# Transposes by DMA in place of TensorE, in an attention with data-dependent decay followed by a SwiGLU FFN

## The chip, the cores and the metric

One core of a Trainium2 chip runs the whole program. The metric is device time in microseconds, the median of several executions.

## The reference

```python
def _attn_ref(r, k, v, w, u):              # (4, 8, 768, 48): batch, heads, time, head size
    for t in range(S):
        cur = np.einsum('bhd,bhe->bhde', u[None] * kt, vt)
        y[:, :, t] = np.einsum('bhd,bhde->bhe', rt, state + cur)
        state = wt[:, :, :, None] * state + np.einsum('bhd,bhe->bhde', kt, vt)

def _moe_ref(x, w_gate, w_val, w_out, rms_g):   # x: (3072, 384); d_ff = 1536
    rms = np.sqrt(np.mean(x * x, axis=-1, keepdims=True) + 1e-06)
    xn = x / rms * rms_g
    g = xn @ w_gate
    silu = g * (1.0 / (1.0 + np.exp(-g)))
    return silu * (xn @ w_val) @ w_out
```

The attention's y, with time and heads put in order (token, head x size), is the FFN's x.

## The kernel before

Time is cut into six blocks of 128 steps (m or n = 0 to 5); each block holds four batches (j = 0 to 3). One batch of one block is a tile with the 128 steps on the partitions and 8 heads x 48 on the free axis. Inside a block the recurrence is done in parallel form: sums of log decay by a matmul with a triangular mask (`cs_mm`), their exponential (`cs_exp`), r and k multiplied by it (`r_mul`, `k_mul`, into bf16 tiles padded to 64 per head so that two heads fill 128 columns), the 128 x 128 products q = k r^T for each head (`q_mm`), masked to earlier steps (`q_mask`), and y = q v + r state (`y_mm`). The diagonal term with u is computed apart: GpSimd multiplies r, k and u (`bonus_mul`), VectorE sums over the head (`bonus_sum`), GpSimd multiplies by v (`bonus_v`), and `x_add` puts it to y. `st_mm` and `st_new` carry the state to the next block.

Products over the head's 48 elements need r and k with the head on the partitions, so `tr_mm` transposes them on TensorE (eight 128 x 128 pieces, two heads each) into PSUM, and ScalarE (`tr_r`) and VectorE (`tr_k`) copy them to `rkT`. In the same way x, once normalised (`x_sq`, `x_rstd` on GpSimd, `xn_mul` with rms_g on VectorE), is transposed in three pieces by `xn_mm` and copied by `xn_out` into `xnt`, the FFN's input for the four batches of a block (512 tokens).

The FFN of block n has 12 steps f (`gv_mm`: six matmuls of 512 columns, `silu` on ScalarE, `h_mul` on VectorE) and four output steps (`o_mm`, 12 matmuls each, `o_out`). PSUM is in three pools of two buffers each: `psG` for cs and gate/value, `psQ` for q and the output, `psT` for transposes, state, y.

The order of all work is a hand-written plan: each operation is entered by `at(time, fn, ...)` with a planned time, the list is sorted, and the operations are issued in that order; every engine and every DMA queue then runs its own part in order, and waits by semaphores. The planned times set the order only. FFN stage n has 16 slots; blocks 0 and 1 are done in a head ahead of FFN 0, and block m from 2 on is done beside FFN m-1, its preparation (cs, r, k, transposes) in the last slots of FFN m-2. The inputs are fp32 and reach SBUF by SP's queue (`load`, L92), in pools of two buffers per input; the weights are cast on the way by GpSimd's queue (`load_gv`, `load_wo`); outputs leave by SP's queue.

Of the kernel before, what the change touches and what calls it, by code (L numbers as in the profile page):

```python
# [25 lines left out]
def kernel(  # L26
# [97 lines left out]
    nc.vector.memset(rA.rearrange("p a b h d -> p (a b h) d")[:, :, D:PD], 0.0)  # L124
    nc.vector.memset(kA.rearrange("p a b h d -> p (a b h) d")[:, :, D:PD], 0.0)
# [57 lines left out]
    def r_mul(n, j):  # L183
        nc.vector.tensor_tensor(out=rA[:, n % 2, j, :, 0:D], in0=inp[n, "r"][:, j],  # L184
                                in1=ewk[n, j][:, 4:4 + DM].rearrange("p (h d) -> p h d", h=H), op=ALU.mult)

    def k_mul(n, j, eng):
        eng.tensor_tensor(out=kA[:, n % 2, j, :, 0:D], in0=inp[n, "k"][:, j],  # L188
                          in1=ewk[n, j][:, 4 + DM:4 + 2 * DM].rearrange("p (h d) -> p h d", h=H),
                          op=ALU.mult)  # L190
# [17 lines left out]
    def tr_mm(n, j):  # L208
        ps = bank["tr", n, j] = psT.tile([128, 2 * NP, 128], BF16, name="ps_t")
        for q in range(NP):  # L210
            nc.tensor.transpose(ps[:, q, :], pair(rA[:, n % 2, j], q), ident)
        for q in range(NP):
            nc.tensor.transpose(ps[:, NP + q, :], pair(kA[:, n % 2, j], q), ident)
        rkT[n, j] = pt.tile([128, 2 * NP, 128], BF16, name="rkT", bufs=5)

    def tr_r(n, j):
        nc.scalar.copy(out=rkT[n, j][:, 0:NP, :], in_=bank["tr", n, j][:, 0:NP, :])  # L217

    def tr_k(n, j):
        nc.vector.tensor_copy(out=rkT[n, j][:, NP:, :], in_=bank["tr", n, j][:, NP:, :])  # L220
# [13 lines left out]
    def q_mask(n, j, half):  # L234
        nc.vector.tensor_tensor(out=qts[n, j][:, half], in0=bank["q", n, j][half],  # L235
                                in1=bc_mid(mask_lt, NP), op=ALU.mult)
# [17 lines left out]
    def y_mm(n, j):  # L254
        if n not in xb:
            xb[n] = pt.tile([128, SB, DM], BF16, name="xb")
            rstd[n] = pt.tile([128, 2, SB], FP32, name="rstd")
        ps = bank["y", n, j] = psT.tile([128, DM], FP32, name="ps_t")
        t, q = rkT[n, j], qts[n, j]
        if n > 0:  # L260
            for i in range(NP):
                nc.tensor.matmul(ps[:, i * 2 * D:(i + 1) * 2 * D], lhsT=t[:, i, :],
                                 rhs=st[:, n % 2, j, i, :], start=(i == 0), stop=False)
        for h in range(H):
            nc.tensor.matmul(ps[:, h * D:(h + 1) * D], lhsT=q[:, h % 2, h // 2, :],  # L265
                             rhs=vb[n][:, j, h, :], start=(n == 0 and h == 0), stop=(h == H - 1))

    def x_add(n, j):
        nc.vector.tensor_tensor(out=xb[n][:, j], in0=bank.pop(("y", n, j)),  # L269
                                in1=ydiag[n][:, j].rearrange("p h d -> p (h d)"), op=ALU.add)  # L270

    def x_sq(n, j):
        nc.scalar.activation(out=junk, in_=xb[n][:, j], func=AF.Square, accum_out=rstd[n][:, 0, j:j + 1])  # L273

    def x_rstd(n, j):
        ss = rstd[n][:, 0, j:j + 1]
        nc.gpsimd.tensor_scalar(out=ss, in0=ss, scalar1=1.0 / DM, scalar2=eps, op0=ALU.mult, op1=ALU.add)
        nc.gpsimd.tensor_tensor(out=rstd[n][:, 1, j:j + 1], in0=ss, in1=mhalf, op=ALU.pow)  # L278

    def xn_mul(n, j):  # L280
        xn = bank["xn", n, j] = pt.tile([128, DM], BF16, name="xn")
        nc.vector.scalar_tensor_tensor(out=xn, in0=xb[n][:, j], scalar=rstd[n][:, 1, j:j + 1],  # L282
                                       in1=g_bc, op0=ALU.mult, op1=ALU.mult)

    def xn_mm(n, j):
        if n not in xnt:
            xnt[n] = pt.tile([128, KC, TS], BF16, name="xnt")
        ps = bank["xt", n, j] = psT.tile([128, KC, 128], BF16, name="ps_t")
        xn = bank.pop(("xn", n, j))
        for c in range(KC):  # L290
            nc.tensor.transpose(ps[:, c, :], xn[:, c * 128:(c + 1) * 128], ident)  # L291

    def xn_out(n, j):
        nc.scalar.copy(out=xnt[n][:, :, j * L:(j + 1) * L], in_=bank.pop(("xt", n, j)))  # L294
# [35 lines left out]
    HEAD = 4.0  # L330
    SLOT = 1.95
    P = 16 * SLOT
    T0 = 3.0 + 8 * HEAD + 4.0

    for m in range(2):
        for j in range(SB):
            t = 3.0 + HEAD * (m * SB + j)
            for i, which in enumerate("wkrv"):
                at(-10 + 0.1 * (m * SB + j) + 0.01 * i, load, m, which, j, 1)
            at(t, ln, m, j, 1)  # L340
            at(t + 0.9, cs_mm, m, j)
# [12 lines left out]
            at(t + 5.0, q_mask, m, j, 1)
            at(t + 5.2, st_mm, m, j)
            at(t + 6.5, y_mm, m, j)
            at(t + 6.7, st_new, m, j)
            at(t + 7.3, x_add, m, j)
            at(t + 7.9, x_sq, m, j)
            at(t + 8.4, x_rstd, m, j)  # L360
            at(t + 9.1, xn_mul, m, j)
            at(t + 9.6, xn_mm, m, j)
            at(t + 9.8, xn_out, m, j)
    at(3.0 + 5 * HEAD, load_gv, 0)
    at(3.0 + 6 * HEAD, load_gv, 1)
    at(3.0 + 7 * HEAD, load_gv, 2)
    at(3.0 + 7 * HEAD + .1, load_wo, 0)
    at(3.0 + 7 * HEAD + .2, load_wo, 1)
    at(3.0 + 7 * HEAD + .3, load_wo, 2)

    for m in range(2, NSB):
        b = T0 + (m - 1) * P
        for i, which in enumerate("wkrv"):
            at(b - 34 * SLOT + 0.01 * i, load, m, which)
        if m == 2:
            at(b - 4 * SLOT - 0.5, ln, m)
            shift, bonus = 0.6, -6
        else:
            at(b - 17 * SLOT + 1.2, ln, m)
            shift, bonus = 0.0, -14  # L380
        at(b - 8 * SLOT, cast_v, m)
        for j in range(SB):
            t = b + (-4 + j) * SLOT + shift
            at(t, cs_mm, m, j)
            at(t + 0.5, cs_exp, m, j)
            at(t + 1.4, r_mul, m, j)
            at(t + 1.4, k_mul, m, j, nc.gpsimd)
            t = b + (bonus + 2 * j) * SLOT
            at(t, bonus_mul, m, j)
            at(t + 3.0, bonus_sum, m, j)  # L390
            at(t + 3.6, bonus_v, m, j)
            t = b + (-2 + j) * SLOT + 0.1
            at(t, tr_mm, m, j)
            at(t + 0.6, tr_r, m, j)
            at(t + 0.6, tr_k, m, j)
            t = b + (1 + 3 * j) * SLOT
            at(t, q_mm, m, j)
            at(t + 0.6, q_mask, m, j, 0)
            at(t + 1.2, q_mask, m, j, 1)
            if m < NSB - 1:  # L400
                at(t + 0.1, st_mm, m, j)
                at(t + 1.8, st_new, m, j)
            t = b + (3 + 3 * j) * SLOT
            at(t, y_mm, m, j)
            at(t + 0.9, x_add, m, j)
            at(t + 1.8, x_sq, m, j)
            at(t + 2.3, x_rstd, m, j)
            t = b + (5 + 3 * j) * SLOT
            at(t, xn_mul, m, j)
            at(t + 0.8, xn_mm, m, j)  # L410
            at(t + 1.4, xn_out, m, j)

    for n in range(NSB):
        b = T0 + n * P
        for f in range(FC):
            t = b + f * SLOT + 0.3
            at(t, gv_mm, n, f)
            at(t + 1.3, silu, n, f)
            at(t + 1.9, h_mul, n, f)
        for j in range(SB):  # L420
            t = b + (FC + j) * SLOT + 0.3
# [35 lines left out]
```

## Time and profile before

| what | value |
|---|---|
| median of 3 runs | 282.22 us (280.76 to 282.44) |
| the profiled execution | 283.02 us, span 281.2 us |
| mean granted TensorE clock | 0.994 |
| TensorE busy | 216.8 us (77%) |
| VectorE, ScalarE, GpSimd busy | 176.9, 136.0, 115.4 us |
| SP's and ScalarE's DMA packets (q1) | 23.60 MB, 42.1% of 16 engines' span |
| GpSimd's DMA packets (q0) | 3.54 MB, 7.9% |

The shares are averages over a head, five stages with attention or a part of it, and a last stage without; a line of a group reads: line, engine, operation, out<-in, count, then busy time and mean ns of one, then the idle time of the engine just before these instructions and what ended it. A row of the timeline reads: start, duration, engine, line. Matmuls overlap, so the distance between starts, not a duration, is what one costs TensorE.

### The profile page before, as it was taken

The page shows a single profiled execution, that of the slowest core. Times are in us where ns is not written, and L with a number is a line of the kernel's source. Part 1 is how long each engine was busy: PE and PEld are TensorE (multiplying, and loading weights), DVE is VectorE, ACT ScalarE, POOL GpSimd, SP SyncE. Part 2 cuts the span into 40 slices and gives each one's busy share as a digit, 9 for nine tenths or more (in the row PEclk, how much of TensorE's full clock was granted, in tenths as well). Part 3 has the DMA queues.
Part 4 walks back from the last instruction along what each step waited for, and adds up shares of the span by engine and source line. Part 5 has one row for each costly group of instructions (what it writes and reads, how often), then busy time and mean ns, then how long its engine had stood idle before and what let it go on. Part 6 is the DMA issues. An engine that isn't in the chain of part 4 may idle for free.

```text
span 281.2 us, 4404 instructions
## 1 busy us (share of the span) xinstructions
PE 216.8 (77%) x1668; PEld 119.1 (42%) x1688; DVE 176.9 (63%) x306; ACT 136.0 (48%) x240; POOL 115.4 (41%) x155
## 2 busy tenths in 40 slices
PE   1355554435899598777998878998779999999994
PEld 0233333323343354333564334664336644554352
DVE  4477777857344235988766788648886578723430
ACT  2344443422445937335666355683447654524420
POOL 2555556592400377566272582644653301110000
PEclk9999999999999979999999999999999999999999
DMA  6999999999990060990069900110000200020002
GB/s 127 200 206 216 187 216 218 206 193 185 219 188 0 0 140 3 224 197 0 0 143 211 211 0 1 59 56 2 0 0 30 85 3 0 2 84 29 2 28 84
DMA packets 106821, 27.81 MB, mean 99 GB/s; under 512 B 99632, under 2 KB 106800, under 8 KB 106800
## 3 DMA queue, kind: packets, MB, share of 16 engines
q1 hardware_dynamic: 102528, 23.60, 42.1%
q0 software_dynamic: 3984, 3.54, 7.9%
q10 hardware_dynamic: 288, 0.39, 0.6%
q8 instruction: 13, 0.21, 0.3%
q14 instruction: 8, 0.07, 0.1%
HBM read 26.35 MB, written 4.72 MB: 110 GB/s over the span
## 4 chain that ended last, share of the span: by engine, by line
PE 34%; DVE 26%; ACT 13%; POOL 8%; SPq 8%; issue 8%; DMA 1%; ACTq 0%; POOLq 0%; DVEq 0%
PE ps_q L317 15%; PE ps_g L303 9%; SPq L92 8%; DVE qts L235 7%; DVE ht L311 6%; DVE xn L282 5%; ACT sg L72 4%; ACT L70 3%; PE ps_t L265 3%; DVE st L250 3%; DVE xb L269 2%; PE ps_t L291 2%; ACT lw L72 2%; POOL ydiag L205 2%; DVE diag L201 2%
## 5 line engine op out<-in xcount | busy, mean ns | idle before, releaser
L311 DVE TENSOR_TENSOR ht<-ps_g,sg 128x512 bf16<-128x512 f32 x72 | 49.5, 690 | 43.5 <-ACT sg L72 43.0
L72 ACT ACTIVATE sg<-ps_g 128x512 bf16<-128x512 f32 x72 | 43.1, 598 | 49.9 <-PE ps_g L303 43.2
L303 PE MATMUL ps_g<-xnt,wg_sb 128*128 128x512 bf16 x203 | 58.3, 385 | 5.1 <-DVE ht L311 3.6
L303 PE MATMUL ps_g<-xnt,wv_sb 128*128 128x512 bf16 x209 | 58.5, 386 | 0.2
L317 PE MATMUL ps_q<-wo_sb,ht 128*128 128x384 bf16 x288 | 51.5, 332 | 3.0 <-DVE ht L311 3.0
L205 POOL TENSOR_TENSOR ydiag<-vt,diag 128x384 f32<-128x384 f32 x24 | 19.9, 830 | 68.1 <-DVE diag L201 67.9
L317 PEld LDWEIGHTS <-ht 128*128 128x128 bf16 x288 | 27.9, 99 | 21.1 <-DVE ht L311 3.4
L235 DVE TENSOR_TENSOR qts<-ps_q,mask_lt 128x512 bf16<-128x512 f32 x48 | 31.4, 683 | 5.6 <-PE ps_q L230 5.6
L303 PEld LDWEIGHTS <-wv_sb 128*128 128x128 bf16 x216 | 21.4, 99 | 26.5 <-issue 1.7
L303 PEld LDWEIGHTS <-wg_sb 128*128 128x128 bf16 x216 | 20.1, 99 | 25.7 <-issue 9.7
L282 DVE SCALAR_TENSOR_TENSOR xn<-xb,rstd,g_bc 128x384 bf16<-128x384 bf16 x24 | 23.5, 978 | 10.3 <-POOL rstd L278 10.1
L294 ACT COPY xnt<-ps_t 128x384 bf16<-128x384 bf16 x24 | 11.5, 479 | 37.7 <-PE ps_t L291 37.7
L188 POOL TENSOR_TENSOR kA<-kt,ewk 128x384 bf16<-128x384 f32 x16 | 18.7, 1171 | 24.6 <-ACT ewk L72 24.5
L72 ACT ACTIVATE ewk<-ps_g 128x772 f32<-128x772 f32 x24 | 19.5, 813 | 18.6 <-PE ps_g L176 18.5
L184 DVE TENSOR_TENSOR rA<-rt,ewk 128x384 bf16<-128x384 f32 x24 | 18.0, 748 | 15.8 <-ACT ewk L72 10.9
L291 PE MATMUL ps_t<-ident,xn 128*128 128x128 bf16 x72 | 9.4, 249 | 23.9 <-DVE xn L282 23.5
L197 POOL TENSOR_TENSOR ruk<-rt,kt 128x384 f32<-128x384 f32 x24 | 24.9, 1038 | 6.8 <-DMA rt<-in_r_dram 6.8
L198 POOL TENSOR_TENSOR ruk<-ruk,u_bc 128x384 f32<-128x384 f32 x24 | 25.7, 1070 | 1.9
L273 ACT ACTIVATE junk<-xb 128x384 bf16<-128x384 bf16 x24 | 12.5, 519 | 14.1 <-DVE xb L269 14.0
L228 PE MATMUL ps_q<-rkT 48*128 48x128 bf16 x96 | 11.3, 247 | 10.2 <-DVE rkT L220 9.7
L220 DVE COPY rkT<-ps_t 128x512 bf16<-128x512 bf16 x24 | 10.1, 422 | 14.2 <-ACT rkT L217 14.0
L291 PEld LDWEIGHTS <-xn 128*128 128x128 bf16 x72 | 4.9, 106 | 32.7 <-DVE xn L282 32.1
(53 smaller groups left out, 294.7 us busy)
## 6 DMA issues: line engine op xcount, KB each, us to landing
out_dram<-ob SPq DMA_DIRECT2D x24, 192.0 KB, 1.9
wt<-in_w_dram SPq DMA_DIRECT2D x4, 768.0 KB, 6.6
kt<-in_k_dram SPq DMA_DIRECT2D x4, 768.0 KB, 7.6
rt<-in_r_dram SPq DMA_DIRECT2D x4, 768.0 KB, 10.4
vt<-in_v_dram SPq DMA_DIRECT2D x4, 768.0 KB, 9.0
wt<-in_w_dram SPq DMA_DIRECT2D x8, 192.0 KB, 3.7
kt<-in_k_dram SPq DMA_DIRECT2D x8, 192.0 KB, 3.9
rt<-in_r_dram SPq DMA_DIRECT2D x8, 192.0 KB, 3.8
```

The source lines that it names most:

```text
L72: nc.scalar.activation(**kw)
L92: nc.sync.dma_start(out=dst, in_=src(t, n, b0, nb))
L188: eng.tensor_tensor(out=kA[:, n % 2, j, :, 0:D], in0=inp[n, "k"][:, j], in1=ewk[n, j][:, 4 + DM:4 + 2 * DM].rearrange("p (h d) -> p h d", ...
L197: nc.gpsimd.tensor_tensor(out=ruk[n][:, j], in0=inp[n, "r"][:, j], in1=inp[n, "k"][:, j], op=ALU.mult)
L198: nc.gpsimd.tensor_tensor(out=ruk[n][:, j], in0=ruk[n][:, j], in1=u_bc, op=ALU.mult)
L205: nc.gpsimd.tensor_tensor(out=ydiag[n][:, j], in0=inp[n, "v"][:, j], in1=diag[n][:, j].to_broadcast([128, H, D]), op=ALU.mult)
L235: nc.vector.tensor_tensor(out=qts[n, j][:, half], in0=bank["q", n, j][half], in1=bc_mid(mask_lt, NP), op=ALU.mult)
L282: nc.vector.scalar_tensor_tensor(out=xn, in0=xb[n][:, j], scalar=rstd[n][:, 1, j:j + 1], in1=g_bc, op0=ALU.mult, op1=ALU.mult)
L291: nc.tensor.transpose(ps[:, c, :], xn[:, c * 128:(c + 1) * 128], ident)
L303: nc.tensor.matmul(ps[:, half * 512:(half + 1) * 512], lhsT=wt[:, c, f * 128:(f + 1) * 128], rhs=xnt[n][:, c, :], start=(c == 0), stop=(c ...
L311: nc.vector.tensor_tensor(out=ht[n][:, f, :], in0=bank.pop(("gv", n, f))[:, 512:1024], in1=bank.pop(("sg", n, f)), op=ALU.mult)
L317: nc.tensor.matmul(ps, lhsT=ht[n][:, f, j * L:(j + 1) * L], rhs=wo_sb[:, f, :], start=(f == 0), stop=(f == FC - 1))
```

## The change

- The r/k transposes go to the DMA engines: r and k share one tile `rk`, and one `dma_start_transpose` per batch (`rk_tr`) writes `rkT` from SBUF to SBUF. `tr_mm`, `tr_r` and `tr_k` are gone.
- The x transposes too (`xn_tr`). In block 0 both kinds are issued from ScalarE's queue, later from SP's.
- rms_g is no longer multiplied along the free axis. x is scaled by its rms on ScalarE (`xn_mul`), transposed, and then multiplied in `xnt` by rms_g as one number per partition (`xn_gain`, three instructions per block on VectorE). rms_g is loaded as 128 x 3 in place of a broadcast to 128 x 384.
- The mask of the odd heads: ScalarE copies q from PSUM (`q_copy_o`) and GpSimd zeroes in place what is not earlier (`q_mask_o`). The even heads' mask stays on VectorE.
- x (`xb`) is kept in fp32 in four buffers, one for each batch; before it was bf16.
- The plan: only block 0 is done ahead of FFN 0, block m from 1 on beside FFN m-1. From block 2 on the inputs are loaded per batch, four loads for each input. FFN slots are planned at 1.65 and output slots at 2.6, before all at 1.95.

```diff
-    rA = persist.tile([128, 2, SB, H, PD], BF16)
-    kA = persist.tile([128, 2, SB, H, PD], BF16)
+    rk = persist.tile([128, 2, SB, 2, H, PD], BF16)
...
-    def tr_mm(n, j):
-        ps = bank["tr", n, j] = psT.tile([128, 2 * NP, 128], BF16, name="ps_t")
-        for q in range(NP):
-            nc.tensor.transpose(ps[:, q, :], pair(rA[:, n % 2, j], q), ident)
-        for q in range(NP):
-            nc.tensor.transpose(ps[:, NP + q, :], pair(kA[:, n % 2, j], q), ident)
+    def rk_tr(n, j, eng=None):
         rkT[n, j] = pt.tile([128, 2 * NP, 128], BF16, name="rkT", bufs=5)
-
-    def tr_r(n, j):
-        nc.scalar.copy(out=rkT[n, j][:, 0:NP, :], in_=bank["tr", n, j][:, 0:NP, :])
-
-    def tr_k(n, j):
-        nc.vector.tensor_copy(out=rkT[n, j][:, NP:, :], in_=bank["tr", n, j][:, NP:, :])
+        (eng or nc.sync).dma_start_transpose(rkT[n, j], rk[:, n % 2, j].rearrange("p c h d -> p (c h d)"))
...
-    def q_mask(n, j, half):
-        nc.vector.tensor_tensor(out=qts[n, j][:, half], in0=bank["q", n, j][half],
+    def q_mask_e(n, j):
+        nc.vector.tensor_tensor(out=qts[n, j][:, 0], in0=bank["q", n, j][0],
                                 in1=bc_mid(mask_lt, NP), op=ALU.mult)
+
+    def q_copy_o(n, j):
+        nc.scalar.copy(out=qts[n, j][:, 1], in_=bank["q", n, j][1])
+
+    def q_mask_o(n, j):
+        nc.gpsimd.affine_select(out=qts[n, j][:, 1], in_=qts[n, j][:, 1], compare_op=ALU.is_gt, fill=0.0,
+                                base=0, pattern=[[0, NP], [1, 128]], channel_multiplier=-1)
...
     def x_add(n, j):
-        nc.vector.tensor_tensor(out=xb[n][:, j], in0=bank.pop(("y", n, j)),
+        xb[n, j] = pt.tile([128, DM], FP32, name="xb", bufs=4)
+        nc.vector.tensor_tensor(out=xb[n, j], in0=bank.pop(("y", n, j)),
                                 in1=ydiag[n][:, j].rearrange("p h d -> p (h d)"), op=ALU.add)
...
     def xn_mul(n, j):
-        xn = bank["xn", n, j] = pt.tile([128, DM], BF16, name="xn")
-        nc.vector.scalar_tensor_tensor(out=xn, in0=xb[n][:, j], scalar=rstd[n][:, 1, j:j + 1],
-                                       in1=g_bc, op0=ALU.mult, op1=ALU.mult)
-
-    def xn_mm(n, j):
+        xn = bank["xn", n, j] = pt.tile([128, DM], BF16, name="xn", bufs=3)
+        nc.scalar.activation(out=xn, in_=xb[n, j], func=AF.Copy, scale=rstd[n, j][:, 1:2])
+
+    def xn_tr(n, j, eng=None):
         if n not in xnt:
             xnt[n] = pt.tile([128, KC, TS], BF16, name="xnt")
-        ps = bank["xt", n, j] = psT.tile([128, KC, 128], BF16, name="ps_t")
-        xn = bank.pop(("xn", n, j))
-        for c in range(KC):
-            nc.tensor.transpose(ps[:, c, :], xn[:, c * 128:(c + 1) * 128], ident)
-
-    def xn_out(n, j):
-        nc.scalar.copy(out=xnt[n][:, :, j * L:(j + 1) * L], in_=bank.pop(("xt", n, j)))
+        (eng or nc.sync).dma_start_transpose(xnt[n][:, :, j * L:(j + 1) * L], bank.pop(("xn", n, j)))
+
+    def xn_gain(n, c):
+        nc.vector.tensor_scalar(out=xnt[n][:, c, :], in0=xnt[n][:, c, :], scalar1=gT[:, c:c + 1],
+                                scalar2=None, op0=ALU.mult)
...
-    for m in range(2):
-        for j in range(SB):
-            t = 3.0 + HEAD * (m * SB + j)
...
+    for j in range(SB):
+        t = 3.0 + 4.0 * j
...
+        at(t + 3.3, rk_tr, 0, j, nc.scalar)
...
+        at(t + 11.4, xn_tr, 0, j, nc.scalar)
...
+                    at(slot(m - 3, i * SB + j) if m > 2 else 30.0 + 4 * i + j, load, m, which, j, 1)
...
+            at(slot(m - 1, x) + 4.0, xn_tr, m, j)
+        for c in range(KC):
+            at(slot(m, 0) - 0.5, xn_gain, m, c)
```

What moves in the issue order is seen best on SP's queue. Before, it held loads alone up to the first output; the rows are the end of the loads of block 1 (8 heads each: one batch), blocks 2 and 3 (32: all four batches) and the first output:

```order
L92 DMA vt<-in_v_dram 128x8x48
L92 DMA wt<-in_w_dram 128x32x48
L92 DMA kt<-in_k_dram 128x32x48
L92 DMA rt<-in_r_dram 128x32x48
L92 DMA vt<-in_v_dram 128x32x48
L92 DMA wt<-in_w_dram 128x32x48
L92 DMA kt<-in_k_dram 128x32x48
L92 DMA rt<-in_r_dram 128x32x48
L92 DMA vt<-in_v_dram 128x32x48
L327 DMA out_dram<-ob 128x384
```

Of the change, the same queue in the second half of FFN 0: loads of r and v of block 3, the four x transposes of block 1 (L281), the first two r/k transposes of block 2 (L208) and the first outputs:

```order
L281 DMA_TRANSPOSE xnt<-xn 128x3x128
L92 DMA kt<-in_k_dram 128x8x48
L92 DMA rt<-in_r_dram 128x8x48 x2
L281 DMA_TRANSPOSE xnt<-xn 128x3x128
L92 DMA rt<-in_r_dram 128x8x48 x2
L92 DMA vt<-in_v_dram 128x8x48
L281 DMA_TRANSPOSE xnt<-xn 128x3x128
L92 DMA vt<-in_v_dram 128x8x48
L318 DMA out_dram<-ob 128x384
L208 DMA_TRANSPOSE rkT<-rk 128x8x128
L92 DMA vt<-in_v_dram 128x8x48
L318 DMA out_dram<-ob 128x384
```

The piece goes on with the second r/k transpose of block 2, the last x transpose of block 1 and the last load of block 3:

```order
L208 DMA_TRANSPOSE rkT<-rk 128x8x128
L281 DMA_TRANSPOSE xnt<-xn 128x3x128
L92 DMA vt<-in_v_dram 128x8x48
L318 DMA out_dram<-ob 128x384
L208 DMA_TRANSPOSE rkT<-rk 128x8x128
```

All of block 2's loads and 15 of block 3's 16 stand ahead of the x transpose that completes FFN 1's input; before, that transpose was no DMA.

On VectorE, at the end of a stage, the last rows of FFN 2 and the first product of FFN 3 (`ht`) before:

```order
L184 TENSOR_TENSOR rA<-rt,ewk 128x8x48
L323 COPY ob<-ps_q 128x384
L184 TENSOR_TENSOR rA<-rt,ewk 128x8x48
L282 SCALAR_TENSOR_TENSOR xn<-xb,rstd,g_bc 128x384
L220 COPY rkT<-ps_t 128x512
L184 TENSOR_TENSOR rA<-rt,ewk 128x8x48
L323 COPY ob<-ps_q 128x384
L220 COPY rkT<-ps_t 128x512
L184 TENSOR_TENSOR rA<-rt,ewk 128x8x48
L220 COPY rkT<-ps_t 128x512
L311 TENSOR_TENSOR ht<-ps_g,sg 128x512
```

and in the change at the same place:

```order
L182 TENSOR_TENSOR rk<-rt,ewk 128x8x48
L199 TENSOR_REDUCE diag<-ruk 128x8
L314 COPY ob<-ps_q 128x384
L182 TENSOR_TENSOR rk<-rt,ewk 128x8x48 x2
L314 COPY ob<-ps_q 128x384
L182 TENSOR_TENSOR rk<-rt,ewk 128x8x48
L284 TENSOR_SCALAR xnt<-xnt,gT 128x512 x3
L302 TENSOR_TENSOR ht<-ps_g,sg 128x512
```

The copies of `rkT` and the products `xn` are gone from VectorE, and the three gains stand last in the stage, ahead of everything that VectorE does for the next one.

More of the change, by code (lines that the diff above doesn't have):

```diff
@@ L364 @@
[L364 to L381, printed above, removed]
-        for j in range(SB):
-            t = b + (-4 + j) * SLOT + shift
+    FS, OS = 1.65, 2.6
@@ new lines @@
+    for c in range(KC):
+        at(T0 - 0.5, xn_gain, 0, c)
+    for i, which in enumerate("wkrv"):
+        at(15.0 + i, load, 1, which)
+    at(15.0, load_gv, 0)
+    at(31.0, load_gv, 1)
+    at(36.0, load_gv, 2)
+    for g in range(3):
+        at(40.0 + g, load_wo, g)
+    for m in range(1, NSB):
+        if m > 1:
+            for i, which in enumerate("wkrv"):
+                for j in range(SB):
+                    at(slot(m - 3, i * SB + j) if m > 2 else 30.0 + 4 * i + j, load, m, which, j, 1)
+        at(22.0 if m == 1 else slot(0, 11.9) if m == 2 else slot(m - 3, 15.5), ln, m)
+        at(slot(m - 1, -6 if m > 1 else 0.5), cast_v, m)
+        for j in range(SB):
+            t = slot(m - 1, -4 + j) if m > 1 else 24.0 + 2 * j
@@ L396 @@
[L396 to L399, printed above, removed]
-            if m < NSB - 1:
[L401 to L409, printed above, removed]
@@ L426 @@
+    for _, _, fn, args in plan:
         fn(*args)
```

144 lines of the change are left out of this document (85 added, 59 removed).

## The prediction

> **What bounds the kernel now.** I read the span by slices first, then the TensorE timeline for the start of each FFN stage, then the stages one by one: which resource is full, and who waits for whom. From the page, the span and the DMA row of the 40 slices (7.03 us each); under it the 82.7 us that this row shows full, as a table by stage:
>
> ```profile
> span 281.2 us, 4404 instructions
> DMA  6999999999990060990069900110000200020002
> ...
> core 0: us, PE busy (x) PEld busy (x) DVE busy (x) ACT busy (x) POOL busy (x), PEclk, DMA share, GB/s
> 1.70:84.40 82.70, 45.04 (x357) 26.40 (x359) 53.00 (x89) 32.10 (x64) 39.24 (x54) 1.00 1.12 201
> ```
>
> Until 84.4 us the 16 DMA engines are full (share 1.12: packets of two queues overlap), while no compute engine is busy for more than 53.0 of 82.7 us. Now the first gate/value matmul of each of the six FFN stages (TensorE timeline):
>
> ```profile
> 71.02 1.06 PE L303 MATMUL ps_g<-xnt,wg_sb 128*128 128x512 bf16 x2 [0.22 <-issue]
> 107.65 0.81 PE L303 MATMUL ps_g<-xnt,wg_sb 128*128 128x512 bf16 x2
> 147.83 0.59 PE L303 MATMUL ps_g<-xnt,wg_sb 128*128 128x512 bf16 x2
> 185.81 0.59 PE L303 MATMUL ps_g<-xnt,wg_sb 128*128 128x512 bf16 x2
> 223.41 0.59 PE L303 MATMUL ps_g<-xnt,wg_sb 128*128 128x512 bf16 x2
> 252.28 0.81 PE L303 MATMUL ps_g<-xnt,wg_sb 128*128 128x512 bf16 x2
> ```
>
> So the kernel is a head of 71.0 us (blocks 0 and 1), a stage of 36.6 (FFN 0), three stages that carry a block's attention beside the FFN (40.2, 38.0, 37.6), one that carries half of it (28.9) and one that is FFN alone (28.9). For the stage from 185.8, the same table, who TensorE waited for, and the groups of instructions that the change touches:
>
> ```profile
> 185.40:223.00 37.60, 32.90 (x288) 18.53 (x290) 28.02 (x50) 20.97 (x39) 18.86 (x24) 1.00 0.06 22
> ...
> PE ps_t L291 <- DVE xn L282: 3.5, 3, 1.7
> PE ps_g L303 <- DVE ht L311: 0.9, 1, 0.9
> ...
> L235 DVE TENSOR_TENSOR qts<-ps_q,mask_lt 128x512 bf16<-128x512 f32 x8 | 5.3, 681 | 0.0
> L282 DVE SCALAR_TENSOR_TENSOR xn<-xb,rstd,g_bc 128x384 bf16<-128x384 bf16 x4 | 3.8, 952 | 1.5 <-POOL rstd L278 1.4
> L205 POOL TENSOR_TENSOR ydiag<-vt,diag 128x384 f32<-128x384 f32 x4 | 3.3, 831 | 10.6 <-DVE diag L201 10.6
> L72 ACT ACTIVATE sg<-ps_g 128x512 bf16<-128x512 f32 x12 | 7.2, 599 | 8.3 <-PE ps_g L303 5.4 <-DVE diag L201 2.0 <-PE ps_t L265 0.9
> L217 ACT COPY rkT<-ps_t 128x512 bf16<-128x512 bf16 x4 | 2.3, 587 | 0.0
> L294 ACT COPY xnt<-ps_t 128x384 bf16<-128x384 bf16 x4 | 1.9, 479 | 6.3 <-PE ps_t L291 6.3
> L220 DVE COPY rkT<-ps_t 128x512 bf16<-128x512 bf16 x4 | 1.7, 422 | 2.6 <-ACT rkT L217 2.6
> ```
>
> Here TensorE is busy 32.9 of 37.6 us, and its largest wait, 3.5 us, is for the normalised x. DMA is idle (0.06). Two kernels in one, then: up to 84 us the queue is the scarce thing, after it TensorE.
>
> **The change, part by part.** *The steady stage.* TensorE loses eight r/k transposes and three x transposes for each of four batches. Their price is the distance between starts:
>
> ```profile
> 182.15 0.33 PE L291 MATMUL ps_t<-ident,xn 128*128 128x128 bf16 x3
> 182.32 0.33 PE L171 MATMUL ps_g<-lw,mask_lt 128*128 128x384 bf16 x1
> ...
> 182.75 0.38 PE L211 MATMUL ps_t<-ident,rA 128*128 128x128 bf16 x4
> 182.97 0.39 PE L213 MATMUL ps_t<-ident,kA 128*128 128x128 bf16 x4
> 183.19 2.11 PE L317 MATMUL ps_q<-wo_sb,ht 128*128 128x384 bf16 x12
> ```
>
> That is 0.17 us for three and 0.44 for eight, 4 x 0.61 = 2.4 us a stage. The wait of 3.5 us for xn goes with the x transposes, since nothing on TensorE reads xn any more. What is late next is xn_gain: three VectorE multiplications over 128x512 stand between the last x transpose's landing and the next stage's first matmul. No such instruction is in the trace; the nearest is the 128x512 copy of L220, 0.42 us, so 3 x 0.42 = 1.3 us at most, and nothing if the transpose lands early. I charge 1.3. The stage becomes 37.6 - 2.4 - 3.5 + 1.3 = 33.0 us; its ends are 31.7 and, if the new waits eat everything, 37.6.
>
> The other engines: VectorE drops four masks (2.7), xn (3.8) and the k copies (1.7), 8.2 of 28.0 us; it was not the bound and I credit nothing beyond the wait above. ScalarE drops 2.3 + 1.9 us of copies and takes four 128x512 copies of the odd masks (0.6 each by L72) and four scalings of x (nearest row below, 0.50): 4.2 against 4.4, no change. GpSimd takes four selects over 128x512; the one in the trace is a quarter of that:
>
> ```profile
> L160 ACT CAST vb<-vt 128x384 bf16<-128x384 f32 x8 | 4.0, 504 | 1.8 <-DMA vt<-in_v_dram 1.8
> L104 POOL TENSOR_SCALAR_AFFINE_SELECT mask_lt<-mask_lt 128x128 bf16<-128x128 bf16 x1 | 0.3, 294 | 0.1
> ```
>
> Between 0.29 and 4 x 0.29 = 1.18 us each, so GpSimd goes from 18.9 to at most 23.6 us of 33: hidden by its idle time. If that cover fails, y_mm waits behind the select (rival B). x in fp32 changes the width of one operand in three instructions of 0.5 us: nothing, or a few tenths either way.
>
> *The two last stages.* FFN 4 loses 4 x 0.17 us of transposes and takes the three gains, 29.5; of the four masks (0.68) and four xn (0.95) that leave VectorE there I credit 1.5, so 28.0. FFN 5 stays 28.9.
>
> *The head and FFN 0.* Only block 0 is left ahead of FFN 0. In the kernel before, block 0's fourth batch had its r ready here, and the first batch's x reached xnt 13.6 us after its r:
>
> ```profile
> 9.06 0.56 DVE L184 TENSOR_TENSOR rA<-rt,ewk 128x384 bf16<-128x384 f32 x1 [4.93 <-DMA rt<-in_r_dram]
> 22.71 0.48 ACT L294 COPY xnt<-ps_t 128x384 bf16<-128x384 bf16 x1 [0.97 <-PE ps_t L291]
> 28.98 0.55 DVE L184 TENSOR_TENSOR rA<-rt,ewk 128x384 bf16<-128x384 f32 x1
> ```
>
> So the compute of block 0 would allow FFN 0 at 29.0 + 13.6 = 42.6 us, 46 with some delay from transposes on ScalarE's queue, and FFN 1 at 46 + 33 to 37, about 80. **This is where the gain shrinks.** The last x transpose of block 1, without which FFN 1 cannot start, stands on SP's queue behind the loads of all of block 2 and of block 3 but the last one (the order pieces in the section on the change show it). Those loads, blocks 0 and 1 and the weights are what kept the DMA engines full until 84.4 us. Less one 192 KB load and the broadcast of rms_g, plus two 192 KB stores that now stand ahead of it, the bytes are the same; and ahead of it stand 10 transposes of r/k and 8 of x, 3/8 as large: 13 r/k transposes' worth. The DMA answers for 0 to 85 us:
>
> ```profile
> q1 hardware_dynamic: 66176, 12.59, 80.4%
> q0 software_dynamic: 3984, 3.54, 26.2%
> ...
> wt<-in_w_dram SPq DMA_DIRECT2D x8, 192.0 KB, 3.7
> ```
>
> No transpose by DMA is in the trace. By pieces: the loads moved 64 x 192 KB in 0.804 x 85 = 68.3 us, 1.07 us for 1024 pieces of 192 bytes (66176 packets / 64); an r/k transpose reads 8 x 128 = 1024 pieces of 256 bytes. As the low end, nothing at all (its packets lie beside another queue's); as the high end, 3.7 us, the landing time of a 192 KB load, as if nothing overlapped. I take 1.07, the row that has its number of pieces: 13 x 1.07 = 13.9 us. FFN 1's x is there at 84.4 + 13.9 + 1.3 (gains) = 99.6 us, some 18 us after FFN 0's own work ends, and TensorE comes to it from idleness, which costs at the start of FFN 0 before:
>
> ```profile
> 71.87 1.49 PE L303 MATMUL ps_g<-xnt,wv_sb 128*128 128x512 bf16 x3
> 78.11 0.81 PE L303 MATMUL ps_g<-xnt,wv_sb 128*128 128x512 bf16 x3
> ```
>
> Three matmuls take 0.7 us longer there, over the first four such groups: about 2.5 us, although the granted clock reads 1.00 up to 84 us.
>
> The Trainium skill has two rules on that term that do not agree (the other stands at rival C). Its page "Advanced Engine Details and Errata", X-Bar Transpose (TRN2), says that such transposes run as fast as plain DMAs, at 350 to 400 GB/s: as an estimate 0.7 us for 256 KB, and the sum would be 5 us lower. No run here shows it yet.
>
> **The sum.** 99.6 + 2.5 + 3 x 33.0 + 28.0 + 28.9 = 258.0 us of span. The profiled execution took 283.02 us beside its span of 281.2, so 1.8 us lie around it: 259.8, say 260. It was 0.8 us above the median of 282.22 and 0.6 above the slowest of the three runs shown; I leave that.
>
> **Rivals.** *A: the queue does not bind.* The transposes lie beside the loads and xn_gain beside the output matmuls. Then FFN 1 starts when the same bytes have landed, 84.4 + 1.3, no idleness precedes it, and the stages take 31.7: 85.7 + 95.1 + 28 + 28.9 = 237.7, with 1.8 about 240. For it: share 1.12 shows that queues overlap. Against: the 82.7 us are full as they stand.
>
> *B: the stage keeps its length.* ScalarE's copy and GpSimd's select now stand in series before y_mm, and GpSimd is a queue in order: it sat 10.6 us of the stage waiting for diag (L205), and a select behind such a wait is late. If it costs TensorE what xn cost, the stages stay at 37.6: 260 + 3 x 4.6 = 274. Against: two matmul slots lie between q_mm and y_mm.
>
> *C: slower than before.* An r/k transpose costs the queue over 2.5 us. Beyond the first stretch, FFN 1 and FFN 2 each need 16 loads (17.1 us), 4 stores (about 4) and 5.5 transposes' worth: more than 33 us from 2.2 us a transpose on. From 1.07 to 2.2 the total rises by 13 a us, to 274.5; from there by 13 + 11 = 24 a us, and passes 283 at 2.55. At 3.7 us it is 274.5 + 1.5 x 24 = 310. For it: 3.7 us is what a smaller load takes to land. Against: at 1.07 us a load, 3.7 us is three to four of them in a row, so the landing counts those ahead. The Trainium skill's page "VectorE: DVE Perf Modes", The three transpose paths, gives 1309 ns for one 128x128 tile by DMA; eight in a row would be, as an estimate, 10.5 us, beyond this rival's whole range. No row here can say whether tiles overlap.
>
> **How the numbers follow.** My sum 0.52 (its own range 248 to 270, for a transpose at 0.3 to 1.8 us and stages of 32 to 34.5); A 0.2; B 0.14; C 0.14, of which 0.03 ends within 1%. A range that leaves out under 2 in 10 runs from 238 to 280. Faster by over 1% (about what a measurement here can tell from no change) 0.87, within 1% 0.03, slower 0.1.
>
> **What would show it.** The DMA row full to about 100 us; a hole in TensorE ahead of FFN 1, ended by VectorE's gain, which waited for DMA; stage starts 33 us apart from there; no TensorE wait for xn; the r/k transposes near 1 us of packet time each. Wrong would be a full DMA row throughout (C), a y_mm that waits for GpSimd (B), or FFN 1 at 86 us (A).

## The result, and the profile after

The changed kernel takes 273.91 us (median of 4 runs, 272.06 to 275.85) beside 282.27 for the kernel before in the same comparison: ratio 0.972 (0.964 to 0.979). It is faster, as forecast, but by 8.4 us in place of 22. Of the runs below, two (block 0 on TensorE, unread transposes) had one slower execution in four, which their medians leave out. The profiled execution took 272.06 us, span 270.3. From its page, TensorE, the granted clock and the DMA row in 40 slices of 6.76 us:

```profile
span 270.3 us, 4039 instructions
...
PE   0123315286729104969799999999999999999994
...
PEclk9999999999977755999999999999999999999999
DMA  6999999799999998699655999969200850120002
```

Before, the DMA row was full to 84.4 us; now it is full, with one dent, to 101 us (slices 1 to 14), and TensorE has a hole of three slices (13 to 15) inside FFN 0, not ahead of FFN 1. The granted clock reads 0.7 and then 0.5 from 74 to 108 us, ahead of and inside that hole, and is full again at FFN 1. The first gate/value matmuls of the six stages on TensorE's timeline (start, duration, in brackets the idle time and what ended it):

```profile
53.65 0.58 PE L294 MATMUL ps_g<-xnt,wg_sb 128*128 128x512 bf16 x1 [3.35 <-DVE xnt L284]
...
119.13 0.90 PE L294 MATMUL ps_g<-xnt,wg_sb 128*128 128x512 bf16 x3 [2.61 <-DVE xnt L284]
...
152.76 0.90 PE L294 MATMUL ps_g<-xnt,wg_sb 128*128 128x512 bf16 x3 [0.56 <-DVE xnt L284]
...
183.92 0.90 PE L294 MATMUL ps_g<-xnt,wg_sb 128*128 128x512 bf16 x3 [0.56 <-DVE xnt L284]
...
215.07 0.90 PE L294 MATMUL ps_g<-xnt,wg_sb 128*128 128x512 bf16 x3 [0.55 <-ACT ob L316]
...
241.97 0.81 PE L294 MATMUL ps_g<-xnt,wg_sb 128*128 128x512 bf16 x3
```

The stages last 65.5, 33.6, 31.2, 31.2, 26.9 and, to the end, 28.3 us. From FFN 1 on everything is as forecast or better; FFN 1 itself starts 11.5 us **later** than before (119.1 against 107.65), where the forecast had 99.6. TensorE's waits from 45 to 120 us (in all, times, longest), and then the chain of what ended last from 94 to 119 us:

```profile
PE ps_g L169 <- ACT lw L72: 17.1, 2, 16.4
PE ps_q L216 <- DMA rkT<-rk: 8.9, 2, 5.9
PE ps_g L294 <- DVE xnt L284: 6.7, 4, 3.3
```
```profile
94.51 4.70 DMA vt<-in_v_dram
...
100.69 0.59 ACT sg L72
...
102.27 1.28 ACT L70
103.57 1.49 ACT lw L72
...
106.01 3.02 PE ps_q L308 x12
...
109.82 1.95 PE ps_q L308 x12
...
116.05 2.65 DMA xnt<-xn
118.72 0.36 DVE xnt L284
```

This is a chain that the forecast did not have. ScalarE casts block 2's v (L158) ahead of the last two silus of FFN 0 and of the ln for block 2 (`lw`, the logarithm of its decay). The cast waited 13.6 us for the last of that v to land, and with it waited all of ScalarE's queue:

```profile
99.31 1.47 ACT L158 CAST vb<-vt 128x1536 bf16<-128x1536 f32 x1 [13.62 <-DMA vt<-in_v_dram]
```

TensorE's queue stood in turn at block 2's cs (L169), which the plan puts ahead of the output matmuls. So the four output steps began at 106, and FFN 1 19.8 us after the cast.

### The profile page after: what moved, and what is told of

Same layout as the page of the kernel before. It is cut to its first block, busy times and chain, and to the rows that moved or that the text cites. A ratio compares the mean times of both kernels' runs of the same rounds, so it can differ in the third digit from the quotient of the medians.

```text
span 270.3 us, 4039 instructions
## 1 busy us (share of the span) xinstructions
PE 192.5 (71%) x1424; PEld 98.7 (37%) x1424; DVE 139.4 (52%) x247; ACT 137.0 (51%) x234; POOL 133.6 (49%) x183
## 4 chain that ended last, share of the span: by engine, by line
PE 43%; DMA 21%; POOL 10%; ACT 8%; DVE 8%; SPq 5%; issue 4%; ACTq 0%; DVEq 0%; POOLq 0%
PE ps_g L294 22%; DMA rkT<-rk 15%; PE ps_q L308 13%; SPq L92 4%; DVE ht L302 3%; PE ps_q L216 3%; DMA xnt<-xn 2%; ACT sg L72 2%; POOL rk L186 2%; DMA wt<-in_w_dram 2%; DMA vt<-in_v_dram 2%; ACT vb L158 2%; POOL ruk L195 2%; POOL ruk L196 2%; DVE rk L186 1%
## 5 line engine op out<-in xcount | busy, mean ns | idle before, releaser
L72 ACT ACTIVATE sg<-ps_g 128x512 bf16<-128x512 f32 x72 | 42.9, 596 | 53.7 <-PE ps_g L294 53.7
L294 PE MATMUL ps_g<-xnt,wg_sb 128*128 128x512 bf16 x216 | 61.6, 392 | 11.2 <-DVE xnt L284 7.9
L308 PEld LDWEIGHTS <-ht 128*128 128x128 bf16 x288 | 28.4, 99 | 18.5 <-issue 1.4
L169 PE MATMUL ps_g<-lw,mask_lt 128*128 128x384 bf16 x24 | 9.2, 385 | 35.7 <-ACT lw L72 33.9
L294 PEld LDWEIGHTS <-wg_sb 128*128 128x128 bf16 x216 | 19.1, 99 | 31.9 <-issue 11.6
L195 POOL TENSOR_TENSOR ruk<-rt,kt 128x384 f32<-128x384 f32 x24 | 24.0, 999 | 13.5 <-DMA rt<-in_r_dram 12.3
L223 DVE TENSOR_TENSOR qts<-ps_q,mask_lt 128x512 bf16<-128x512 f32 x24 | 16.4, 683 | 27.3 <-PE ps_q L218 22.3
L230 POOL TENSOR_SCALAR_AFFINE_SELECT qts<-qts 128x512 bf16<-128x512 bf16 x24 | 16.0, 668 | 27.7 <-ACT qts L227 27.7
L182 DVE TENSOR_TENSOR rk<-rt,ewk 128x384 bf16<-128x384 f32 x24 | 18.2, 762 | 21.0 <-ACT ewk L72 20.9
L271 POOL TENSOR_SCALAR rstd<-rstd 128x1 f32<-128x1 f32 x24 | 5.7, 237 | 46.9 <-ACT junk L267 46.4
L186 POOL TENSOR_TENSOR rk<-kt,ewk 128x384 bf16<-128x384 f32 x20 | 24.1, 1210 | 4.8 <-ACT ewk L72 4.7
L72 ACT ACTIVATE ewk<-ps_g 128x772 f32<-128x772 f32 x24 | 19.4, 813 | 10.1 <-PE ps_g L174 9.8
L227 ACT CAST qts<-ps_q 128x512 bf16<-128x512 f32 x24 | 13.9, 579 | 15.8 <-PE ps_q L218 13.7
L216 PEld LDWEIGHTS <-rkT 48*128 48x128 bf16 x96 | 6.0, 102 | 32.3 <-DMA rkT<-rk 24.2
L199 DVE TENSOR_REDUCE diag<-ruk 128x8 f32<-128x384 f32 x24 | 13.1, 546 | 8.9 <-POOL ruk L196 8.9
```

The costliest lines, as they stand in the source:

```text
L72: nc.scalar.activation(**kw)
L182: nc.vector.tensor_tensor(out=rk[:, n % 2, j, 0, :, 0:D], in0=inp[n, "r"][:, j], in1=ewk[n, j][:, 4:4 + DM].rearrange("p (h d) -> p h d", ...
L186: eng.tensor_tensor(out=rk[:, n % 2, j, 1, :, 0:D], in0=inp[n, "k"][:, j], in1=ewk[n, j][:, 4 + DM:4 + 2 * DM].rearrange("p (h d) -> p h d ...
L195: nc.gpsimd.tensor_tensor(out=ruk[n][:, j], in0=inp[n, "r"][:, j], in1=inp[n, "k"][:, j], op=ALU.mult)
L216: nc.tensor.matmul(qe[:, i, :], lhsT=t[0:D, NP + i, :], rhs=t[0:D, i, :], start=(i == 0), stop=(i == NP - 1))
L223: nc.vector.tensor_tensor(out=qts[n, j][:, 0], in0=bank["q", n, j][0], in1=bc_mid(mask_lt, NP), op=ALU.mult)
```

## The experiments

Two theories came first. **Packet time** (P; in later expectations volume or queue time): the transposes cost more time of the DMA queue than the 1.07 us charged. **Order** (O): FFN 0 cannot end before loads for which its own queues wait, so too many bytes stand ahead of FFN 1. After the first four runs a third was set against packet time: **blocking**, that a transpose which waits for its operands holds the loads behind it in SP's queue.

For several runs the transposes of some blocks were put back on TensorE, with the copies of the kernel before; a transpose whose PSUM buffer would not be free at its place in the plan is issued at the next place where it is:

```diff
+    def plan_rk(t, n, j, eng=None):
+        if PE_RK(n):
+            at(t, tr_mm, n, j)
+            at(t + 0.6, tr_r, n, j)
+            at(t + 0.6, tr_k, n, j)
+        else:
+            at(t, rk_tr, n, j, eng)
...
-            at(t + 2.9, rk_tr, m, j)
+            plan_rk(t + 2.9, m, j)
```

`plan_x` does the same for x. The runs, with the start of FFN 0 and FFN 1 in the profiled execution and the cast of block 2's v where it waited for its DMA:

| kernel | median us | ratio to before (95%) | FFN 0 | cast | FFN 1 |
|---|---|---|---|---|---|
| changed | 273.91 | 0.972 (0.964 to 0.979) | 53.7 | 99.31 | 119.1 |
| all on TensorE | 274.73 | 0.972 (0.967 to 0.977) | 52.8 | 80.57 | 103.0 |
| blocks 0, 1 on TensorE | 254.56 | 0.901 (0.898 to 0.905) | 52.8 | 80.25 | 99.4 |
| cast late | 270.38 | 0.958 (0.954 to 0.962) | 55.8 | moved | 115.4 |
| block 3's loads late | 285.81 | 1.014 (1.008 to 1.019) | 56.4 | 90.63 | 110.3 |
| block 1 on TensorE | 259.47 | 0.920 (0.917 to 0.924) | 62.9 | no wait | 105.4 |
| block 0 on TensorE | 262.22 | 0.927 (0.920 to 0.935) | 46.2 | 88.75 | 108.1 |
| blocks 0, 1 on TensorE, cast late | 248.53 | 0.881 (0.877 to 0.885) | 52.9 | moved | 93.7 |
| old order, by DMA | 283.91 | 1.007 (1.004 to 1.009) | 89.0 | – | 123.6 |
| unread transposes | 265.82 | 0.943 (0.936 to 0.951) | 56.7 | 91.26 | 110.1 |
| unread copies | 260.17 | 0.924 (0.918 to 0.930) | 55.6 | 86.47 | 105.7 |
| x by DMA | 256.29 | 0.911 (0.906 to 0.916) | 51.7 | 82.10 | 101.5 |
| block 1 by ScalarE's queue | 272.17 | 0.966 (0.960 to 0.972) | 56.6 | 95.92 | 119.3 |

**All transposes on TensorE** (`PE_RK` and `PE_X` true for all n; new order, masks and gains kept).

> The new plan, the new masks and gains, but every transpose back on TensorE (two psT buffers, copies by ScalarE and VectorE). Two theories of why FFN 1 started at 119.1 us and not at 99.6. P (packet time): the transposes take 1.5 us of the DMA engines and up to 2.4 beside other queues, not 1.07, and 13 r/k transposes' worth stand ahead of FFN 1's x. O (order): FFN 0 cannot finish before the loads that its own rows wait for (the cast of block 2's v stands ahead of the last two silus on ScalarE), and blocks 1 to 3 and the weights are too many bytes ahead of it. P expects FFN 1 at about 100 us, stages from there of 34 to 36 (2.4 us of transposes and a new copy each): 262 to 268 in all. O expects FFN 1 at 110 to 119 and a total of 272 to 282.

274.73 us, what the changed kernel takes: in this order moving the transposes was worth nothing in all. It gives 5.4 us in each of the stages FFN 2 and 3 (36.6 to 31.2) and loses 16.2 us ahead of FFN 1. What made the kernel faster than before is the new order with its masks and gains. P had the start of FFN 1 nearly right (103.0 for about 100) and the total wrong, since FFN 1 takes 40.3 us and the next two 36.6, not 34 to 36. O had the total, but by a start at 110 to 119 that did not come: luck.

**Blocks 0 and 1 on TensorE** (`n < 2`).

> Only blocks 0 and 1 are transposed on TensorE, 8 r/k and 8 x transposes fewer on the queues until FFN 1; blocks 2 to 5 by DMA as in the change. P expects FFN 1 at about 101 us and the stages unchanged at 31 to 34: 253 to 258 in all. O expects FFN 1 at 110 to 119: 264 to 274.

Both halves at once: 254.56 us. FFN 1 starts 19.8 us earlier, and FFN 2 and 3 take 31.2 each, as P expected and O did not. But FFN 1 does not start at 85.7, where the forecast's bytes alone would have put it. ScalarE's cast in this kernel:

```profile
80.25 1.47 ACT L158 CAST vb<-vt 128x1536 bf16<-128x1536 f32 x1 [4.71 <-DMA vt<-in_v_dram]
```

The v is there at 80.25, near the end of the full queue before (84.4); FFN 1 follows 19.1 us later. So the transposes delay v by 19.1 us, and the order theory is right about another 19 us behind it.

**The cast late.**

```diff
-        at(slot(m - 1, -6 if m > 1 else 0.5), cast_v, m)
+        at(slot(m - 1, (-0.2 if m == 2 else -6) if m > 1 else 0.5), cast_v, m)
```

> The change, with one operation moved in the plan: the cast of block 2's v, which waited until 99.3 us for its load with two silus of FFN 0 behind it on ScalarE, comes at the end of FFN 0 in place of slot 10. O expects the output matmuls of FFN 0 to start near 92 instead of 105.8 us and FFN 1 at 104 to 110: 255 to 265 in all. P expects little: the last x transpose of block 1 stands behind the same packets, FFN 1 at 115 or later, 268 to 274.

The output steps begin at 91.3 in place of 106, as O expected, yet FFN 1 gains only 3.8 us, as P expected:

```profile
115.35 1.46 PE L294 MATMUL ps_g<-xnt,wg_sb 128*128 128x512 bf16 x3 [12.90 <-DVE xnt L284]
```

That is the wait that the forecast had in mind, for block 1's x behind SP's queue: the last x was ready at 102.0, and SP issued its transpose at 112.1. In the changed kernel both chains end within 4 us of each other, so either alone buys little.

**Block 3's loads late** (its 16 loads moved from FFN 0 into FFN 1, its ln and bonus after them).

> The change, with block 3's 16 loads (17 us of queue by the 1.07 of the loads before) moved from FFN 0 into FFN 1, and its log and bonus to the places that block 2 has relative to its stage. If bytes ahead of FFN 1's input are what counts, whichever theory, FFN 1 comes 6 us earlier (six of these loads stand ahead of block 2's v) to 15 us earlier (15 stand ahead of the last x transpose): 104 to 113 us, and FFN 2 starts 33 to 38 us later if the loads hide there: 255 to 270 in all. Slower than 274 if block 3's late loads hold up FFN 1 as block 2's did FFN 0.

v is there at 90.63, 8.7 us earlier, and FFN 1 at 110.3, as expected; but the loads do not hide. FFN 1 takes 51.9 us and FFN 2 34.8, since the cast of block 3's v now waits on ScalarE inside FFN 1, as block 2's did in FFN 0:

```profile
142.95 1.47 ACT L158 CAST vb<-vt 128x1536 bf16<-128x1536 f32 x1 [13.88 <-DMA vt<-in_v_dram]
```

The bytes are put off, not saved.

**Block 1 alone, block 0 alone on TensorE** (`n == 1`, `n == 0`).

> The changed kernel with the transposes of block 1 alone on TensorE (four of r and k, four of x); block 0 and blocks 2 to 5 by DMA. Both blocks together gave back 19.8 us of the start of FFN 1 (119.1 to 99.4). Volume theory: what counts is how much queue time the transposes take, whichever block they belong to. Half of them is gone, so FFN 1 starts near 109 and the time is 263 to 265. Blocking theory: a transpose that waits for its own operands holds SP's queue in order, and the loads of block 2 and 3 stand behind it; block 1's transposes are the ones on SP's queue, block 0's are on ScalarE's. Then nearly all comes back: FFN 1 at 99 to 103, time 254 to 258.

> The mirror image: only block 0's transposes on TensorE, those of block 1 still on SP's queue. Volume theory: FFN 1 starts near 109, time 263 to 265, as with block 1 alone. Blocking theory: FFN 1 starts at 115 to 119, time 270 to 274, and only the start of FFN 0 gains (53.7 to about 52).

Each gives over half: FFN 1 at 105.4 and 108.1, together 24.8 us for the 19.8 of both. The run with block 0 decides: blocking had 115 to 119 there, so it is not the whole cause. The run with block 1 lies between the theories, 2.4 us from the 103 of blocking and 3.6 from the 109 of volume, so a part of it stays possible. TensorE's waits up to the start of FFN 0 with block 1 alone on TensorE show what else block 0's transposes cost, since FFN 0 starts at 62.9 there and at 52.8 with block 0's on TensorE too:

```profile
PE ps_q L216 <- DMA rkT<-rk: 14.4, 4, 6.9
```

TensorE waits for the landing in all four batches of block 0.

**Blocks 0 and 1 on TensorE, and the cast late.**

> Blocks 0 and 1 transposed on TensorE, and the cast of block 2's v moved behind FFN 0's last silus. With the transposes by DMA that cast moved late only traded one wait for another (FFN 1 at 115.4 for 119.1), since the x transposes of block 1 then ended last, behind SP's loads. Here those are gone, so if the cast is what holds FFN 0's silus until block 2's last v has landed, the 7.8 us that TensorE waits for ln before the output matmuls go: FFN 1 at 91 to 95, time 247 to 251. If the loads hold FFN 1 by another road too (a DMA that block 1's own rows need), the time stays at 253 to 255.

As expected: 248.53 us, FFN 1 at 93.7. TensorE's wait for ln falls from 7.8 us (first row, the run of 254.56 us) to 2.5:

```profile
PE ps_g L169 <- ACT lw L72: 7.8, 1, 7.8
...
PE ps_g L169 <- ACT lw L72: 2.5, 1, 2.5
```

This is the fastest version here, 25 us under the changed kernel and 34 under the kernel before.

**The old order with the transposes by DMA** (the changed kernel's operations, the plan of before: blocks 0 and 1 ahead of FFN 0, slots of 1.95; loads somewhat later).

> The transposes by DMA, the masks and the gains of the changed kernel, but in the order of the kernel before: blocks 0 and 1 whole ahead of FFN 0, slots of 1.95. Loads of later blocks are issued a little later than there. If the dear part is queue time of the transposes in the first stretch, whatever the order, then FFN 0 starts late, at 80 to 92 instead of 71.0, and the stages behind it are near 33: 264 to 275. If the loss comes from the new order alone, FFN 0 starts at 71 to 75, and the time is 258 to 264.

283.91 us, slower than both theories said and 0.7% slower than before. FFN 0 starts 18.0 us later than before, as the first theory had it, and TensorE waited in the head, up to 92 us, for every one of the eight batches:

```profile
PE ps_q L216 <- DMA rkT<-rk: 57.8, 8, 10.8
```

The stages behind it take 34.6, 36.9, 33.3, 33.0, 26.9 and 28.6 us, 193.4 against 210.2 before: 16.8 us won, 18.0 lost. The 16.8 hold the masks and the gains too; no run takes these apart in the old order. In either order the transposes by DMA win little or nothing, because the first two blocks pay what the others win.

**Unread transposes** (blocks 0 and 1 on TensorE, and the eight r/k transposes issued by DMA besides, at their old places and queues).

```diff
+    def unread(n, j, eng=None):
+        t = pt.tile([128, 2 * NP, 128], BF16, name="unread", bufs=5)
+        (eng or nc.sync).dma_start_transpose(t, rk[:, n % 2, j].rearrange("p c h d -> p (c h d)"))
```

> Blocks 0 and 1 transposed on TensorE, as in the run of 254.6 us, and beside that the eight r/k transposes by DMA issued again, on the queues and at the places of the changed kernel, into a tile that nothing reads. No instruction waits for them. Queue-time theory: the cost is time that a transpose takes from the transfers behind it. From a quiet stretch of the changed kernel (207 to 222 us: 9.2 us of queue time, less 0.45 for one x transpose and 0.5 for each of three stores, over four r/k transposes) that is 1.5 to 1.8 us each, eight of them 12 to 14 us: FFN 1 starts at 109 to 114 instead of 99.4, and the time is 264 to 269. Latency theory: the cost is what TensorE waits for a transpose to land. Nothing waits here, so FFN 1 starts at 99 to 101 and the time is 254 to 257.

```profile
91.26 1.47 ACT L158 CAST vb<-vt 128x1536 bf16<-128x1536 f32 x1 [11.88 <-DMA vt<-in_v_dram]
```

Nothing reads them, and v comes 11.0 us later than without: 1.38 us each, FFN 1 at 110.1, time 265.82, as queue time has it; latency, with FFN 1 at 99 to 101, falls. A transpose must still wait for its r and k, with SP's loads behind it: SP's queue stood 5.1 us ahead of these transposes and 5.7 us ahead of the copies below. So what such waits cost is in both prices, about alike, and their difference is the transpose's own.

**Unread copies** (the same tiles by a plain `dma_start`).

> The same with eight plain copies by DMA of the same 256 KB from SBUF to SBUF, in place of the unread transposes. If the price is one of bytes, or of any write into SBUF beside the loads: the same as the unread transposes. If it is the small pieces of a transpose that are dear, these copies cost 256/192 of the 0.5 us that a 192 KB store took alone, 0.7 us each: FFN 1 at 103 to 106, time 258 to 261.

```profile
86.47 1.47 ACT L158 CAST vb<-vt 128x1536 bf16<-128x1536 f32 x1 [8.07 <-DMA vt<-in_v_dram]
```

6.2 us for eight, 0.78 each, near the 0.7 expected: for the same bytes a transpose takes 1.8 times a copy inside SBUF. It is not the bytes alone. Beside the loads it is no dearer: their 1.07 us for 192 KB would be 1.43 for 256 KB.

**x by DMA** (`PE_RK` for n < 2, `PE_X` never).

> r and k of blocks 0 and 1 transposed on TensorE, all x by DMA. An x transpose alone in the queue took 0.45 us (190 to 207 us of the changed kernel: 8.0% of 17 us for three), eight of them 3.6 us. Queue-time theory: FFN 1 starts at 101 to 104 instead of 99.4, time 255 to 260. Blocking theory: an x transpose that waits for its xn holds SP's queue with block 3's loads behind it, or lands behind the loads ahead of it, and FFN 1 starts at 107 to 113, time 262 to 268.

```profile
82.10 1.47 ACT L158 CAST vb<-vt 128x1536 bf16<-128x1536 f32 x1 [8.55 <-DMA vt<-in_v_dram]
```

The x transposes cost 1.9 us at v and 2.1 at FFN 1, in place of 3.6 for eight from the packets of three in a quiet stretch of the changed kernel (190 to 207 us; share of 16 engines):

```profile
q1 hardware_dynamic: 1287, 0.30, 8.0%
```

But SP issued the last load of that v at 77.90 and block 1's first x transpose at 79.92, so only block 0's four stand ahead of v: 0.46 us each, the 0.45 of the packets. Blocking, with FFN 1 at 107 to 113, falls here.

**Block 1's transposes on ScalarE's queue.**

```diff
-            at(t + 2.9, rk_tr, m, j)
+            at(t + 2.9, rk_tr, m, j, nc.scalar if m == 1 else None)
...
-            at(slot(m - 1, x) + 4.0, xn_tr, m, j)
+            at(slot(m - 1, x) + 4.0, xn_tr, m, j, nc.scalar if m == 1 else None)
```

> The changed kernel with the transposes of block 1 issued from ScalarE's queue instead of SP's; nothing else differs. Queue-time theory: they take the same time from the 16 engines wherever they are issued, and ScalarE pays 1.25 us to issue each of eight: FFN 1 at 115 to 124, time 270 to 280. Blocking theory: SP's loads no longer wait behind a transpose that waits, and a transpose no longer lands behind SP's loads: FFN 1 at 103 to 110, time 258 to 265.

272.17 us, FFN 1 at 119.3: the numbers that queue time had. The cast runs 3.4 us earlier, so SP's order had some part in it, but that is lost again at FFN 1, at the wait for x:

```profile
119.28 1.46 PE L294 MATMUL ps_g<-xnt,wg_sb 128*128 128x512 bf16 x3 [5.35 <-DVE xnt L284]
```

More differs than the expectation had, so the run does not decide between the theories. Block 1's last x was ready at 111.1, but ScalarE issued its transpose only at 115.56, when an r/k transpose of block 2 from SP's queue had landed (chain of what ended last); and SP's loads still stood behind transposes, for up to 8.2 us at once:

```profile
111.64 3.83 DMA rkT<-rk
115.47 0.02 issue
115.49 0.04 ACTq L281
...
SPq L92 <- DMA rkT<-rk: 15.5, 3, 8.2
```

## Why the prediction was wrong, step by step

*FFN 1's start, 99.6 forecast, 119.1 measured: the step that failed.* It was the sum 84.4 + 13.9 + 1.3. In its place the runs show 80.2 + 19.1 + 19.8; the misses are -4.2, +5.2 and +18.5. Behind FFN 1's start 7.2 us came back, so that the span missed by 12.3 only.

- The bytes. Without the transposes the last v of block 2 is there at 80.2, so 84.4 was near.
- The transposes, 13.9. They delay v by 19.1 us, of which 11.0 are what the eight of r/k cost unread and 1.9 those of x. The other 6.2 are for the most part a slower queue. Up to the landing of v the changed kernel moved 97.5 us x 176 GB/s = 17.2 MB, and with blocks 0 and 1 on TensorE 78.5 us x 186 GB/s = 14.6 MB. The 2.6 MB between them take 13.9 us at 186 GB/s; the lower rate costs the other 5.2 (the changed kernel first; the last figure of a row is GB/s; below them a wait of SP's queue in the changed kernel):

```profile
1.70:99.20 97.50, 39.33 (x288) 18.34 (x288) 40.36 (x64) 31.74 (x55) 46.19 (x61) 0.92 1.24 176
1.70:80.20 78.50, 44.96 (x370) 25.18 (x370) 41.70 (x72) 38.43 (x69) 46.51 (x61) 1.00 1.18 186
...
SPq L208 <- DMA xnt<-xn: 6.0, 2, 4.2
```

The last row is a part of it: from 45 to 51 us SP's queue stood ahead of block 1's first r/k transpose until the x transposes from ScalarE's queue had landed, and from 46 to 52 us the engines moved 89 GB/s (192 with blocks 0 and 1 on TensorE). How the 5.2 us divide further is not isolated. That the 13.9 of the bytes meets the forecast's 13.9 is luck: the forecast counted 13 r/k transposes' worth at 1.07 us, and 9.5 (eight and 4 x 3/8) stand ahead of v, at 1.38 us by the unread ones. The price by pieces was 0.31 too low; by bytes at the loads' rate it would have been 1.43. Taken alone, this term would have cost 5 us.
- The tail, 1.3 for the gains: **the large miss.** The forecast ended FFN 0 at about 80 whatever the loads did, and had only x and its gains behind the queue. But FFN 0's own rows wait for block 2: a cast of v ahead of its last two silus on ScalarE, a cs ahead of its outputs on TensorE. So the last silus, the ln, four output steps and block 1's last x come after the load. The distance from the cast to FFN 1 is 19.8, 19.1, 18.8, 19.3, 19.4, 19.3 and 19.7 us in seven kernels (the changed one, blocks 0 and 1, unread transposes, unread copies, x by DMA, block 0, block 3 late), while the cast moves from 80 to 99. (It is 22.4 with all transposes on TensorE, and 23.4 with block 1's on ScalarE's queue, where x ends the wait.) The plan said so: it put preparation of block m into FFN m-2, and loads for it into the one stretch where the queue was full. The forecast read SP's order there, not ScalarE's or TensorE's. The cast is not the whole of it: with the cast late and blocks 0 and 1 on TensorE, FFN 0 still ran from 52.9 to 93.7, where the forecast had 46 to 80.

*The cold start, 2.5 forecast.* FFN 1 takes 33.6 us, FFN 2 and 3 take 31.2, so the size is met by luck: the cause is another. By stages (TensorE busy first, the clock ahead of the DMA share):

```profile
119.13:152.76 33.63, 30.43 (x244) 16.12 (x245) 22.19 (x44) 21.01 (x37) 25.23 (x32) 1.00 0.81 143
152.76:183.92 31.16, 30.09 (x244) 16.06 (x245) 21.46 (x42) 22.26 (x39) 21.68 (x28) 1.00 1.08 184
183.92:215.07 31.15, 30.08 (x244) 16.04 (x245) 21.46 (x42) 21.10 (x39) 21.66 (x28) 1.00 0.42 85
```

Only 0.3 us of it is longer matmuls, at a clock of 1.00; the other 2.1 us TensorE spends waiting.

*The stages, 33.0 forecast, 31.2 measured.* The x wait of 3.5 and the transposes of 2.4 went as forecast; of the 1.3 for the gains 0.56 is left (the wait at the stage's start above), and the far end of 31.7 was about right. TensorE is busy for 30.1 of 31.2 us, whether the queue is full (1.08) or not. *The last two*, 28.0 and 28.9, were 26.9 and 28.3. From FFN 1 to the end the forecast had 158.4 us, the run 151.2.

*The rivals.* A fell: the transposes do not hide. B named 274, the time measured, by a road that is not there: y_mm's waits for the select are 4.2 us in the whole span.

```profile
PE ps_t L257 <- POOL qts L230: 4.2, 7, 0.7
```

C fell: an r/k transpose costs 1.4 us of queue, not over 2.5. On the price of eight tiles the Trainium skill's page "VectorE: DVE Perf Modes", The three transpose paths, gave 1309 ns for one 128x128 tile, as an estimate 10.5 us for eight in a row; here the eight of one transpose land after 3.0 us at the least, 3.9 in the median, so the eight do not follow one another at that price:

```profile
DMA to landing us min/median/max: 3.0/3.9/18.9
```

The rule of "Advanced Engine Details and Errata", X-Bar Transpose (TRN2), in the Trainium skill, that such a transpose runs as fast as a plain DMA, does not hold in this kernel against a copy inside SBUF: 1.38 us against 0.78 for the same bytes. Against the loads it does: 1.43 us for these bytes at their rate.

## What to carry to other kernels

Ahead of moving work to the DMA engines, find the stretches in which they are full and price them there: here the transposes of a block won 5.4 us in a stage where the queue had room and cost about 10 us where it had none, and splitting the choice by block won both (254.6 against 273.9 and 274.7). When a resource is late, don't stop at who waits for it last: on each engine's queue look at the first instruction that needs it, and count all that stands behind, since a preparation placed early for a later stage makes the present stage wait for the later stage's loads. And where two chains end within a few us, one change alone shows little (3.5 us for the late cast with all transposes by DMA, 6.0 with the first two blocks' on TensorE).

## What had not been expected of the hardware

A transpose by DMA that lands in 3.0 us in a quiet stretch took up to 18.9 us beside the weights' transfers (GpSimd's queue, 74.8% of the 16 engines from 60 to 80 us): from 60.27 us on, SP's queue was held for 8.8 us at issuing it.

```profile
60.27 8.79 SPq L208 DMA_TRANSPOSE rkT<-rk  x1
```

Issuing one took SP 1.29 us in the median, where a load took about 0.6 in the quiet stretch. And transposes from two queues waited for one another: SP issued its first at 51.12 us, when the last from ScalarE's queue, issued at 47.29, had landed after 3.8 us.
